# Attention through memory slots with a mixture of depths: factor stores on ScalarE in a new layout, row loads shared by SP and POOL, the mean added on VectorE

## The chip, the cores and the metric

The kernel runs on one core of a Trainium2 chip. A core has five engines that run their own instruction queues in order: TensorE (PE, with its weight loads PEld), VectorE (DVE), ScalarE (ACT), GpSimd (POOL) and SyncE (SP); transfers are done by 16 DMA engines, and each transfer is issued as an instruction in the queue of some engine. An order between engines exists only where one waits for a semaphore of another. The metric is the device time of one run in microseconds (us). The span, from the first to the last instruction of one profiled execution, is a little shorter than that execution's own device time.

## The reference

Sizes: B = 8 batches, H = 8 heads, S = 576 tokens, Dh = 64, M = 32 memory slots, D = 512, F = 1024, capacity 128; all float32.

```python
a    = softmax(phi, axis=2)                      # over the S tokens, for each of 32 slots
k_m  = einsum('bhsm,bhsd->bhmd', a, k)           # key means, 32 x 64 per head
v_m  = einsum('bhsm,bhsd->bhmd', a, v)           # value sums, 32 x 64 per head
x    = softmax(q @ k_m.T / 8, axis=-1) @ v_m     # then heads side by side: (B, S, 512)
scores  = x @ w_gate
top_idx = argpartition(-scores[b], 128)[:128]    # per batch
out     = x.copy()
out[b, top_idx] = x[top_idx] + sigmoid(scores[top_idx]) * (relu(x[top_idx] @ w1) @ w2)
```

The choice of the 128 tokens is made by comparing scores, so that x has to be computed more exactly than its own tolerance would ask; that is why the kernel splits its numbers into high and low parts.

## The kernel before

**Tiling and stages.** The 8 x 8 heads are 16 groups of 4 heads (batch b, half g). Four heads of 32 slots fill the 128 partitions, and S lies along the free dimension. A group passes these stages, each a Python generator whose `yield` ends a step:

- `softmax` (L187-282), the exponential worked out in many VectorE and ScalarE instructions on 128 x 576 tiles. L215, L245, L253, L262 and L278 are some of VectorE's; `dh` (L231), `vh` (L234), `y0` and `inv` are ScalarE's, all through the helper `act` (L181).
- `keys` (L306-337): TensorE transposes the factors a (L314), ScalarE copies them to SBUF (L316), VectorE splits them into `hi` (L320) and `lo` (L322). POOL then stores both to the DRAM buffer `aparts[4, B, 2, 2, S, M]` with eight DMAs (L325), one for each part and head, each of 576 contiguous pieces of 128 B. TensorE multiplies k with a in 24 matmuls (L331) for the key means, and ScalarE copies these to `kbd` (L336).
- `split_v` (L284-302) loads v of a group (`vb`, L291), splits it on VectorE (L294, L296), and stores the parts to the DRAM buffer `vparts` from POOL (L298). Its pool `vio` has two buffers for the first nine groups; later `vio2` has one and each group is done in two cuts.

**Value sums.** They are made for sets of SET = 2 batches (four groups), in pieces of T = 18 of the 576 rows: 32 pieces a set, 128 in all. `load_rows` (L341) reads a piece back from DRAM in five DMAs, all issued by SP: one of `v_rows` (L344, 64 partitions, 288 KB) and four of `a_rows` (L351, one per head, 36 KB each, 16 partitions). There are three buffers of each. `all_sums` (L355) loads up to three pieces ahead, and starts on a set when the youngest of its four groups was finished at least five turns ago (L367, `made + 5`). A piece is 72 small matmuls on TensorE (L382) that add into four accumulators; after a set ScalarE copies them to `v_m` (L393).

**Per batch.** When the sums of a batch are there, `attention` runs: `centre` (L405) subtracts means (L417 is one of its VectorE steps; POOL makes the casts `los`, L443 and L445), `scores` (L482) multiplies q with the key means and takes the exponential (`expm1`, L477 and L479), and `attend` (L527) multiplies by `v_m` (denominators L535, products L548), scales by the reciprocal on VectorE (L552), adds the mean's row (L555; on POOL while softmaxes are still running, which the variable `working` tells, and on VectorE after that), computes the gate's scores, and stores x to `out` (L560) and to the scratch buffer `xs` (L564) from POOL's queue. `rank` (L574, L601) finds each token's rank, `gather` (L611) fetches the 128 chosen rows by an indirect DMA of POOL (L630), and `ffn` (L636) does the two products (L654, L664) and scatters the result (L671). At the end a value is loaded that tells whether a general path, not taken here, must be run.

**What sets the order.** The program is scheduled by hand: each engine executes in the order in which the Python code emits. The main loop (L753-786) goes by turns. In a turn come: one step of a softmax or `keys`, where two chains of groups alternate (`order`, L112: groups 0, 2, 4, 6, 8, 9, ... 15 and groups 1, 3, 5, 7, so that from the eighth on a single chain runs); every fourth turn, or every second once attention has begun (`attend_all`), a step of `split_v` (L763); 12, 10 or 7 steps of the sums, two time steps of a piece each (`steps`, L730); a step of attention; and two of the feed-forward part. `load_phi` (L98), `load_k` (L102, called at L228 inside `softmax`) and `load_q` (L106, called at L683 between `scores` and `attend`) bring inputs in from SP's queue. At turn 40 the two weight matrices are loaded (L758, L759).

Of the kernel before, what the change touches and what calls it, by code (L numbers as in the profile page):

```python
# [39 lines left out]
def kernel(  # L40
# [26 lines left out]
    F = w1.shape[1]  # L67
    KD, KF = D // P, F // P
    SET = 2
    T = 18  # L70
    scale = 1.0 / Dh ** 0.5
    out_flat = out.rearrange("b s d -> (b s) d")

# [28 lines left out]
    def load_k(i, ch):  # L102
        ks[i] = exs[ch].tile([PT, NC, D // NG], F32, name="kb")
        nc.sync.dma_start(out=ks[i], in_=k[groups[i]])
# [82 lines left out]
    def softmax(i, ch):  # L187

        ex = exs[ch]

        def t(name, dtype=F32):

            return ex.tile([P, NC * P if name in WIDE else S], dtype, name=name)[:, :S]

        r = phis.pop(i)
        less_mx = ex.tile([P, 1], F32, name="mx")
        nc.vector.tensor_scalar(out=t("den"), in0=r, scalar1=-1.0, scalar2=None, op0=ALU.mult,
                                op1=ALU.min, accum_out=less_mx)
        nc.scalar.activation(r, r, AF.Identity, bias=less_mx)
        q = t("q", I16)  # L200
        act(q, r, LOG2E)
        yield
        for ln2 in (LN2_HI, LN2_LO):
            stt(out=r, in0=q, scalar=-ln2, in1=r, op0=ALU.mult, op1=ALU.add)

        rh, rl = t("rh", I16), t("rl")
        act(rh, r, 2.0 ** 11)
        num, den = t("num"), t("den")
        act(num, r, SQ[0], SQ[1], AF.Square)
        act(den, r, EXP_Q[2] * UP, EXP_Q[1] * UP)  # L210
        ends = t("lo"), t("big")
        act(ends[0], rh, -0.2734375 * UP * GRID, UP)
        act(ends[1], rh, UP * GRID / 4, EXP_P[1] * UP)
        yield
        stt(out=num, in0=num, scalar=SQ[2], in1=r, op0=ALU.add, op1=ALU.mult)  # L215
        act(num, num, 1.0, EXP_P[2] * UP)
        stt(out=rl, in0=rh, scalar=-GRID, in1=r, op0=ALU.mult, op1=ALU.add)

        def near(val, f, end):


            low = t("low")
            stt(out=low, in0=val, scalar=-f * UP, in1=r, op0=ALU.add, op1=ALU.mult)
            stt(out=low, in0=rl, scalar=f * UP, in1=low, op0=ALU.mult, op1=ALU.add)
            tt(out=val, in0=end, in1=low, op=ALU.add)

        yield
        load_k(i, ch)  # L228
        near(den, -0.2734375, ends[0])
        dh = t("dh", I16)  # L230
        act(dh, den, FINE)  # L231
        near(num, 0.25, ends[1])
        vh = t("vh", I16)
        act(vh, num, GRID)  # L234
        y0 = t("y0", I16)
        act(y0, r, 1.0, 14 * LN2, AF.Exp)
        inv = t("rl2")
        act(inv, r, INV[0], INV[1], AF.Exp)
        act(inv, inv, 1.0, INV[2] - 9 * LN2, AF.Exp)
        yield  # L240


        lo, big, low = t("lo"), t("big"), t("low")
        tt(out=low, in0=num, in1=rl, op=ALU.mult)
        stt(out=lo, in0=num, scalar=GRID, in1=vh, op0=ALU.mult, op1=ALU.subtract)  # L245
        tt(out=lo, in0=lo, in1=rh, op=ALU.mult)
        tt(out=big, in0=vh, in1=rh, op=ALU.mult)
        tt(out=low, in0=low, in1=lo, op=ALU.add)
        stt(out=num, in0=big, scalar=UP, in1=low, op0=ALU.add, op1=ALU.add)
        yield  # L250

        dl, p = t("lo"), t("big")
        stt(out=dl, in0=den, scalar=FINE, in1=dh, op0=ALU.mult, op1=ALU.subtract)  # L253
        tt(out=p, in0=y0, in1=dh, op=ALU.mult)
        tt(out=num, in0=num, in1=p, op=ALU.subtract)
        tt(out=dl, in0=y0, in1=dl, op=ALU.mult)
        tt(out=num, in0=num, in1=dl, op=ALU.subtract)
        two_q = t("den", I32)
        yield
        act(two_q, q, UP, 127 * UP, AF.Relu)  # L260
        tt(out=num, in0=num, in1=inv, op=ALU.mult)
        tt(out=num, in0=num, in1=y0, op=ALU.add)  # L262
        sm = ex.tile([P, 4], F32, name="sm")
        e = num
        stt(out=e, in0=num, scalar=FINE, in1=two_q.bitcast(F32),
            op0=ALU.mult, op1=ALU.mult, accum_out=sm[:, 0:1])

        nc.vector.tensor_scalar_add(sm[:, 0:1], sm[:, 0:1], 1e-9)
        nc.vector.reciprocal(sm[:, 1:2], sm[:, 0:1])
        nc.vector.tensor_single_scalar(sm[:, 2:3].bitcast(I32), sm[:, 0:1].bitcast(I32), -4096,  # L270
                                       op=ALU.bitwise_and)
        nc.vector.tensor_sub(sm[:, 3:4], sm[:, 2:3], sm[:, 0:1])
        nc.vector.tensor_scalar_mul(sm[:, 2:3], sm[:, 2:3], -1.0)
        a0 = t("vh", F16)
        nc.scalar.activation(a0, e, AF.Copy, scale=sm[:, 1:2])  # L275
        yield
        for part in (2, 3):
            stt(out=e, in0=a0, scalar=sm[:, part:part + 1], in1=e, op0=ALU.mult, op1=ALU.add)  # L278
        stt(out=e, in0=e, scalar=sm[:, 1:2], in1=a0, op0=ALU.mult, op1=ALU.add)  # L279
        soft[i] = e  # L280
        yield
        yield from keys(i, ch)

    def split_v(some, pool, cuts):  # L284

        n = 4 * S * Dh // P
        for b, g in some:
            for x0 in range(0, n, n // cuts):
                x = slice(x0, x0 + n // cuts)
                vb = pool.tile([P, n // cuts], F32, name="vb")  # L290
                nc.sync.dma_start(out=vb, in_=v[b, g, :, x])  # L291
                yield
                hi = pool.tile([P, n // cuts], F32, name="vhi")
                nc.vector.tensor_single_scalar(hi.bitcast(I32), vb.bitcast(I32), -4096,  # L294
                                               op=ALU.bitwise_and)
                nc.vector.tensor_sub(vb, vb, hi)  # L296
                for vp, src in enumerate((vb, hi)):
                    nc.gpsimd.dma_start(  # L298
                        out=vparts[b, g, :, vp].rearrange("w r s d -> w (r s d)")
                                               .rearrange("w (p x) -> p w x", p=P)[:, :, x],  # L300
                        in_=src.unsqueeze(1).to_broadcast([P, 2, n // cuts]))
                yield
# [3 lines left out]
    def keys(i, ch):  # L306
# [13 lines left out]
        nc.vector.tensor_single_scalar(hi.bitcast(I32), aS.bitcast(I32), -4096,  # L320
                                       op=ALU.bitwise_and)
        nc.vector.tensor_sub(lo, aS, hi)  # L322
        for part, src in enumerate((lo, hi)):
            for h in range(4):
                nc.gpsimd.dma_start(  # L325
                    out=aparts[h, b, g, part].rearrange("(c p) m -> p c m", p=PT),
                    in_=src[:, :, h * M:(h + 1) * M])
        km = bank([P, 2, 2 * M])
        for rr in range(2):
            for c in range(NC):  # L330
# [3 lines left out]
        for u in range(2):  # L334
            part = slice(u * Dh, (u + 1) * Dh)
            nc.scalar.activation(kbd[b][part, 2 * g:2 * g + 2, u * M:(u + 1) * M],  # L336
                                 km[part, :, u * M:(u + 1) * M], AF.Copy)

    accs = [accp.tile([P, 512], F32, name=f"acc{i}") for i in range(2 * SET)]

    def load_rows(k, st, ch):  # L341
# [4 lines left out]
            in_=vparts[some].rearrange("b g t w r s d -> (b g t w r) (s d)")  # L346
                [:, ch * T * Dh:(ch + 1) * T * Dh])
        for h in range(4):
            src = aparts[h, some].rearrange("b g t s m -> (b g t) (s m)")
            src = src[:, ch * T * M:(ch + 1) * T * M]  # L350
            nc.sync.dma_start(  # L351
                out=a_rows[k % 3][2 * h::8, h].rearrange("p s m -> p (s m)").bitcast(F32),
                in_=src.unsqueeze(1).to_broadcast([4 * SET, 2, T * M]))

    def all_sums():  # L355
# [7 lines left out]
        def load_some(end):  # L363
            while len(loaded) < min(end, len(pieces)):
                st, ch = pieces[len(loaded)]

                if not all(turn >= made.get(i, turn) + 5  # L367
                           for i in range(st * SET * NG, (st + 1) * SET * NG)):
                    break
                load_rows(len(loaded), st, ch)  # L370
# [156 lines left out]
    def attend(b, general):  # L527
        eT, tg = eTs[b % 2], tgs[b % 3]
        row, rest = mean[b]
        for c0 in range(0, NT, 2):  # L530
# [5 lines left out]
                                     rhs=heads_of, start=True, stop=True)  # L536
            if working:
                yield
            rd = step.tile([P, 2, H], F32, name="rd")[:, :cols]
            nc.vector.tensor_scalar(out=rd.rearrange("p c (g h) -> p c g h", g=2), in0=den,  # L540
                                    scalar1=float(M), scalar2=1e-9, op0=ALU.add, op1=ALU.add)
# [2 lines left out]
            for c in range(cols):  # L544
                o = bank([P, D])
                nc.tensor.matmul(out=o, lhsT=ones3, rhs=rest, start=True, stop=False)
                for g in range(2):
# [4 lines left out]
                nc.vector.tensor_mul(x[:, c].rearrange("p (h d) -> p h d", d=Dh),  # L552
                                     o.rearrange("p (h d) -> p h d", d=Dh),
                                     rd[:, c].unsqueeze(2).to_broadcast([P, H, Dh]))
            (nc.gpsimd if working else nc.vector).tensor_add(  # L555
                x, x, row.unsqueeze(1).to_broadcast([P, cols, D]))
            yield
            score(tg[:, c0:c0 + cols, 1], x, cols)
# [117 lines left out]
    def attention(b, general=False):  # L676
# [2 lines left out]
        yield from (scores_less_max if general else scores)(b)  # L679
        for j in range(2):  # L680
            yield
            if not general and b + 1 < B:
                load_q(b + 1, j)  # L683
        yield from attend(b, general)
        yield
        yield from rank(b)
# [66 lines left out]
    while True:  # L753
# [6 lines left out]
        if working and next(working[0], working) is working:  # L760
            finish(working[1])
            working.clear()
        if working and turn % (2 if attend_all else 4) == 1:  # L763
            next(working[1], None)
        for _ in range(steps()):
            next(sums, None)
        if attend_all is None and set(order[1]) <= set(made):
# [4 lines left out]
                ctx.enter_context(tc.tile_pool(name=name, bufs=2 - (name == "one"),  # L772
                                               reuse_waits="tile"))
                for name in ("step", "work", "one"))
            vio = ctx.enter_context(tc.tile_pool(name="vio2", bufs=1, reuse_waits="tile"))
            working[1] = split_v(groups[two + 1:], vio, 2)
            for j in range(2):
                load_q(0, j)
# [58 lines left out]
```

## Time and profile before

| | before |
|---|---|
| median of 3 runs (lowest to highest) | 908.98 us (899.76 to 917.44) |
| profiled execution: own time | 899.93 us |
| its span | 898.1 us |
| busy PE / PEld | 584.2 us (65%) / 427.7 us (48%) |
| busy DVE | 611.5 us (68%) |
| busy ACT / POOL | 295.3 us (33%) / 234.9 us (26%) |
| mean granted TensorE clock | 0.822 |
| moved by DMA | 166.10 MB, mean 185 GB/s |

The busy times are sums over the whole span, and the stages differ. The borders of the stages are events of the trace: the key means of groups 0 to 3 are ready at 49.4, 78.0, 106.5 and 135.0 us, the value sums of the four sets at 291, 431, 614 and 774 us, and the key means of the last group at 641 us. In a row of a group, "idle before" is the time for which the engine stood just ahead of these instructions, and the name after the arrow is what ended it. In a row of the timeline come the start, the duration, the engine and line, the operation with what it writes and reads, and in brackets the wait ahead of it and what ended that; a name ending in q (SPq) is a queue's issuing instruction.

### The profile page before, as it was taken

The numbers are of one execution on the slowest core, as the hardware profiler recorded it, in microseconds if no ns is written. First come the engines' busy times: TensorE is split into PE (matmuls) and PEld (weight loads), VectorE is DVE, ScalarE is ACT, GpSimd is POOL, SyncE is SP. The second block draws the span as 40 slices with busy tenths as digits, with TensorE's granted clock in tenths as the row PEclk, the third lists the DMA queues.
The fourth block names the chain that finished last, engine by engine and source line by source line (L and its number), as shares of the span: only waits on it lengthen the run. The fifth ranks groups of instructions, "written<-read, shape, count | busy, mean of one in ns | idle before, by whom it ended". The sixth has DMA issues, their size and how long they took to land. (4 is left out here: it accounts for less than half of the span.)

```text
span 898.1 us, 25253 instructions
## 1 busy us (share of the span) xinstructions
PE 584.2 (65%) x10738; PEld 427.7 (48%) x10738; DVE 611.5 (68%) x1117; ACT 295.3 (33%) x578; POOL 234.9 (26%) x349
## 2 busy tenths in 40 slices
PE   0122322556764646695847889867889989888794
PEld 0012222456653535574714557555556577544441
DVE  4899888857874765779789685979845333537820
ACT  3434434324441513332433624343331310332130
POOL 7033311330220432151423314232511010112200
PEclk9999999757585776886667979985899977989597
DMA  6367936876857786788554778664256566123300
GB/s 169 144 198 271 312 124 204 274 250 176 253 154 241 231 259 186 254 289 254 181 186 139 221 210 256 201 191 138 71 171 195 181 202 204 58 77 117 117 25 15
DMA packets 61944, 166.10 MB, mean 185 GB/s; under 512 B 11136, under 2 KB 21376, under 8 KB 61824
## 3 DMA queue, kind: packets, MB, share of 16 engines
q1 hardware_dynamic: 40096, 94.14, 34.8%
q0 software_dynamic: 21728, 70.27, 23.7%
q8 instruction: 87, 1.43, 0.7%
q14 instruction: 33, 0.27, 0.1%
HBM read 96.21 MB, written 68.16 MB: 183 GB/s over the span
## 5 line engine op out<-in xcount | busy, mean ns | idle before, releaser
L382 PE MATMUL acc<-a_rows,v_rows 32*64 32x128 f32 x9216 | 214.3, 253 | 127.8 <-DMA a_rows<-aparts 121.4
L382 PEld LDWEIGHTS acc<-a_rows,v_rows 32*64 32x64 f32 x9216 | 193.5, 162 | 170.4 <-issue 83.0
L314 PE MATMUL bank<-ident,num 128*96 128x128 f32 x96 | 21.3, 386 | 104.4 <-DVE num L279 99.4
L331 PE MATMUL bank<-lo,kb 96*128 96x64 f32 x384 | 64.5, 345 | 20.0 <-ACT lo L316 20.0
L331 PEld LDWEIGHTS bank<-lo,kb 96*128 96x128 f32 x384 | 62.7, 257 | 25.5 <-ACT lo L316 22.4
L325 POOL DMA_DIRECT2D aparts<-low x64 | 46.9, 740 | 104.8 <-DVE low L322 89.7
L298 POOL DMA_DIRECT2D vparts<-vb x23 | 16.9, 735 | 217.8 <-DVE vb L296 217.8
L654 PE MATMUL bank<-w_sb,xeT 128*128 128x512 f32 x128 | 69.8, 679 | 4.9 <-ACT xeT L645 3.2
L314 PEld LDWEIGHTS bank<-ident,num 128*96 128x96 f32 x96 | 15.4, 178 | 108.8 <-issue 88.4
L664 PE MATMUL bank<-w_sb,hT 128*128 128x512 f32 x128 | 60.8, 609 | 0.0
L548 PE MATMUL bank<-vbd,eT 128*128 128x256 f32 x160 | 58.3, 499 | 0.0
L552 DVE TENSOR_TENSOR xj<-bank,rd 128x512 f32<-128x512 f32 x40 | 27.5, 688 | 32.9 <-PE bank L548 32.4
L601 DVE SCALAR_TENSOR_TENSOR cmp<-row,tg,wide 128x576 bf16<-128x576 f32 x40 | 32.5, 814 | 24.0 <-ACT row L587 23.1
L325 POOL DMA_DIRECT2D aparts<-big x64 | 46.5, 734 | 3.8 <-DMA vparts<-vhi 3.7
L548 PEld LDWEIGHTS bank<-vbd,eT 128*128 128x128 f32 x160 | 34.1, 236 | 16.0 <-issue 12.1
L654 PEld LDWEIGHTS bank<-w_sb,xeT 128*128 128x128 f32 x128 | 25.3, 215 | 30.6 <-issue 22.1
L275 ACT ACTIVATE vh<-num,sm 128x576 f16<-128x576 f32 x16 | 12.4, 776 | 78.2 <-DVE sm L270 63.1
L555 POOL TENSOR_TENSOR xj<-xj,mean 128x1024 f32<-128x1024 f32 (+1 forms) x11 | 23.6, 2147 | 49.5 <-DVE xj L552 41.6
L479 DVE SCALAR_TENSOR_TENSOR eT<-es,th 128x288 f32<-128x288 f32 x32 | 14.4, 450 | 31.9 <-ACT th L477 31.9
L664 PEld LDWEIGHTS bank<-w_sb,hT 128*128 128x128 f32 x128 | 22.5, 189 | 25.9 <-issue 24.4
L336 ACT ACTIVATE kbd<-bank 64x64 f32<-64x64 f32 x32 | 7.0, 218 | 83.5 <-PE bank L331 83.3
L560 POOL DMA_DIRECT2D out<-xj x24 | 16.3, 678 | 66.8 <-DVE xj L555 63.8
(149 smaller groups left out, 1155.8 us busy)
## 6 DMA issues: line engine op xcount, KB each, us to landing
v_rows<-vparts SPq DMA_DIRECT2D x128, 288.0 KB
a_rows<-aparts SPq DMA_DIRECT2D x512, 36.0 KB
vparts<-vb POOLq DMA_DIRECT2D x9, 1152.0 KB, 5.5
vparts<-vhi POOLq DMA_DIRECT2D x9, 1152.0 KB, 8.7
kb<-in_k SPq DMA_DIRECT2D x16, 576.0 KB
qb<-in_qT SPq DMA_DIRECT2D x16, 576.0 KB
out<-xj POOLq DMA_DIRECT2D x16, 512.0 KB, 4.1
xs<-xj POOLq DMA_DIRECT2D x16, 512.0 KB, 4.3
```

The costliest lines, as they stand in the source:

```text
L298: nc.gpsimd.dma_start(out=vparts[b, g, :, vp].rearrange("w r s d -> w (r s d)") .rearrange("w (p x) -> p w x", p=P)[:, :, x], in_=src.unsq ...
L314: nc.tensor.transpose(out=tp[:, c], in_=a[:, (c0 + c) * PT:(c0 + c + 1) * PT], identity=ident)
L325: nc.gpsimd.dma_start(out=aparts[h, b, g, part].rearrange("(c p) m -> p c m", p=PT), in_=src[:, :, h * M:(h + 1) * M])
L331: nc.tensor.matmul(out=km[:, rr], lhsT=kb[:, c, rr * P:(rr + 1) * P], rhs=aS[:, c, rr * 2 * M:(rr + 1) * 2 * M], start=(c == 0), stop=(c = ...
L382: nc.tensor.matmul(out=accs[i][:Dh, :P].rearrange("p (h m) -> p h m", m=M), lhsT=vr[p, s], rhs=ar[p, :, s], start=(ch == 0 and s == 0), st ...
L548: nc.tensor.matmul(out=o[:, g * 4 * Dh:(g + 1) * 4 * Dh], lhsT=eT[:, g, (c0 + c) * P:(c0 + c + 1) * P], rhs=vbd[b % 3][:, g], start=False, ...
L552: nc.vector.tensor_mul(x[:, c].rearrange("p (h d) -> p h d", d=Dh), o.rearrange("p (h d) -> p h d", d=Dh), rd[:, c].unsqueeze(2).to_broadc ...
L555: (nc.gpsimd if working else nc.vector).tensor_add(x, x, row.unsqueeze(1).to_broadcast([P, cols, D]))
L560: nc.gpsimd.dma_start(out=out[b, c0 * P:c0 * P + (cols - 1) * P + n].rearrange("(c p) d -> p c d", p=n), in_=x[:n])
L601: nc.vector.scalar_tensor_tensor(out=cmp, in0=row, scalar=g, in1=wide[:, off:off + S], op0=ALU.is_equal, op1=ALU.mult, accum_out=equal[:, ...
L654: nc.tensor.matmul(out=ps[:n], lhsT=xeT[:, d, :n], rhs=w1_sb[:, d, f0:f0 + 512], start=(d == 0), stop=(d == KD - 1))
L664: nc.tensor.matmul(out=ps[:n], lhsT=hT[:, f, :n], rhs=w2_sb[:, f], start=(f == 0), stop=(f == KF - 1))
```

## The change

It has these parts.

- *Factors' layout and stores.* `aparts` becomes `(B, 2, 2, NC, 4, PT, M)`: batch, half, part, chunk of 96 rows, head, row, slot. The eight stores of a group become two, one per part, each from 96 partitions with 24 pieces of 128 B per partition. ScalarE issues them instead of POOL, and they stand after the copies to `kbd` instead of before the key matmuls.
- *Row loads.* T goes from 18 to 16, so that a piece lies within a chunk of 96 rows, and there are 36 pieces a set, 144 in all. Of the four `a_rows` loads of a piece, heads 0 and 1 stay on SP and heads 2 and 3 go to POOL; `v_rows` stays on SP. A set may start four turns after its last group, not five.
- *The split of v.* Its stores go from POOL to ScalarE, a turn's `yield` stands between the subtraction and the stores, `vio2` has two buffers, and once attention runs its steps come in two turns of three (before: one of two); ahead of that, one of three (before: one of four).
- *The mean.* L555 is a VectorE instruction throughout.
- *Input loads.* `load_k` is called one step later in `softmax`; `load_q` of the next batch is called inside `attend`, after its first denominators.

```diff
-    T = 18
+    T = 16
+    assert PT % T == 0
...
         yield
-        load_k(i, ch)
         near(den, -0.2734375, ends[0])
...
         stt(out=num, in0=big, scalar=UP, in1=low, op0=ALU.add, op1=ALU.add)
         yield
+        load_k(i, ch)
...
                 nc.vector.tensor_sub(vb, vb, hi)
+                yield
                 for vp, src in enumerate((vb, hi)):
-                    nc.gpsimd.dma_start(
+                    nc.scalar.dma_start(
...
         nc.vector.tensor_sub(lo, aS, hi)
-        for part, src in enumerate((lo, hi)):
-            for h in range(4):
-                nc.gpsimd.dma_start(
-                    out=aparts[h, b, g, part].rearrange("(c p) m -> p c m", p=PT),
-                    in_=src[:, :, h * M:(h + 1) * M])
         km = bank([P, 2, 2 * M])
...
                                  km[part, :, u * M:(u + 1) * M], AF.Copy)
+        for part, src in enumerate((lo, hi)):
+            nc.scalar.dma_start(
+                out=aparts[b, g, part].rearrange("c h p m -> p (c h) m"),
+                in_=src.rearrange("p c (h m) -> p (c h) m", m=M))
...
         for h in range(4):
-            src = aparts[h, some].rearrange("b g t s m -> (b g t) (s m)")
-            src = src[:, ch * T * M:(ch + 1) * T * M]
-            nc.sync.dma_start(
+            src = aparts[some, :, :, ch * T // PT, h].rearrange("b g t p m -> (b g t) (p m)")
+            src = src[:, ch * T % PT * M:(ch * T % PT + T) * M]
+            (nc.sync if h < 2 else nc.gpsimd).dma_start(
                 out=a_rows[k % 3][2 * h::8, h].rearrange("p s m -> p (s m)").bitcast(F32),
                 in_=src.unsqueeze(1).to_broadcast([4 * SET, 2, T * M]))
...
-                if not all(turn >= made.get(i, turn) + 5
+                if not all(turn >= made.get(i, turn) + 4
...
             if working:
                 yield
+            if c0 == 0 and not general and b + 1 < B:
+                for j in range(2):
+                    load_q(b + 1, j)
...
-            (nc.gpsimd if working else nc.vector).tensor_add(
+            nc.vector.tensor_add(
                 x, x, row.unsqueeze(1).to_broadcast([P, cols, D]))
...
         for j in range(2):
             yield
-            if not general and b + 1 < B:
-                load_q(b + 1, j)
...
-        if working and turn % (2 if attend_all else 4) == 1:
+        if working and (turn % 3 if attend_all else turn % 3 == 1):
             next(working[1], None)
...
-            vio = ctx.enter_context(tc.tile_pool(name="vio2", bufs=1, reuse_waits="tile"))
+            vio = ctx.enter_context(tc.tile_pool(name="vio2", bufs=2, reuse_waits="tile"))
...
-    aparts = nc.dram_tensor("aparts", (4, B, H // 4, 2, S, phi.shape[3]), F32, kind="Internal").ap()
+    aparts = nc.dram_tensor("aparts", (B, H // 4, 2, NC, 4, PT, phi.shape[3]), F32, kind="Internal").ap()
```

## The prediction, made before the changed kernel was run

> **What bounds the kernel now.** I read the busy time by stage first. The stage borders are events in the trace: key means of the first four groups ready (L336 at 135 us), set sums done (L393 at 291, 431, 614 and 774 us), last softmax done (641 us).
>
> ```profile
> core 0: us, PE busy (x) PEld busy (x) DVE busy (x) ACT busy (x) POOL busy (x), PEclk, DMA share, GB/s
> 0.00:137.00 137.00, 27.51 (x120) 24.98 (x120) 110.52 (x172) 55.51 (x89) 47.41 (x92) 1.00 0.62 201
> 137.00:291.00 154.00, 83.20 (x2432) 76.26 (x2433) 113.32 (x184) 51.66 (x83) 31.35 (x45) 0.70 0.73 224
> 291.00:431.00 140.00, 93.43 (x2499) 77.87 (x2498) 103.19 (x191) 46.25 (x92) 42.10 (x58) 0.73 0.77 241
> ...
> 460.00:614.00 154.00, 119.30 (x2613) 83.68 (x2611) 123.69 (x227) 61.58 (x121) 51.46 (x63) 0.86 0.68 207
> ...
> 650.00:776.00 126.00, 117.32 (x2566) 81.63 (x2565) 51.50 (x108) 25.93 (x67) 16.25 (x27) 0.89 0.60 181
> 776.00:898.00 122.00, 94.00 (x328) 50.20 (x326) 58.41 (x140) 32.61 (x77) 18.18 (x31) 0.84 0.20 65
> ```
>
> To 641 us the softmax chain on VectorE sets the pace (110 of 137 us, then 113 of 154); after that TensorE does (117 of 126). VectorE has slack between 137 and 614 us. Where it goes is seen by following its longest idle stretch back, from the stretches of the timeline on VectorE, ScalarE and TensorE:
>
> ```profile
> 197.44 0.48 PE L382 MATMUL acc<-a_rows,v_rows 32*64 32x128 f32 x8 [7.76 <-DMA a_rows<-aparts]
> 203.27 0.45 ACT L336 ACTIVATE kbd<-bank 64x64 f32<-64x64 f32 x2 [15.51 <-PE bank L331]
> 205.03 0.76 DVE L245 SCALAR_TENSOR_TENSOR lo<-num,vh 128x576 f32<-128x576 f32 x1 [10.87 <-ACT vh L181]
> ```
>
> A row load comes late, TensorE stands at the sums (L382), the key matmuls queued behind them are late, ScalarE stands at the copy L336, and VectorE at L245. And the rows are late because SP's queue does nothing but issue:
>
> ```profile
> 211.87 0.50 SPq L344 DMA_DIRECT2D v_rows<-vparts  x1
> 212.41 2.45 SPq L351 DMA_DIRECT2D a_rows<-aparts  x4
> 214.96 0.50 SPq L344 DMA_DIRECT2D v_rows<-vparts  x1
> 215.51 2.44 SPq L351 DMA_DIRECT2D a_rows<-aparts  x4
> ```
>
> A piece every 3.1 us, of which 2.95 is issue. Adding up VectorE's idle stretches over 1 us from 137 to 641 us by their releasers, about 56 us hang on rows in this way (10.9, 4.6, 7.8, 2.9, 2.1, 11.2, 2.6, 3.1, 6.4, 4.9 us), 9 us on vb from HBM (4.9, 1.6, 2.6), and 6.7 us on POOL's add (2.5, 4.2).
>
> **What the Trainium skill says.** Perfetto Trace Analysis, "DMA Instruction — HWDGE (DVE, Sync)": an SP or ACT queue is held until all descriptors of its DMA are generated, and the two share one generator. The trace before agrees so far as it goes: a load with 512 contiguous pieces (qb, 128 partitions x 4) holds SP for 0.6 us, one with 1024 (w2, L759) for 1.16:
>
> ```profile
> 82.83 1.16 SPq L759 DMA_DIRECT2D w_sb<-in_w  x1
> ...
> 364.40 0.61 SPq L108 DMA_DIRECT2D qb<-in_qT  x1
> ```
>
> Against it: w1 (L758), also 512 pieces but of 4 KB, held it for 1.19. SBUF — State Buffer, "Who interferes with whom": a VectorE instruction with two SBUF inputs contends with a GpSimd one that reads SBUF. The trace agrees: L215 takes 0.76 us by its median, and beside POOL's add
>
> ```profile
> 397.40 2.36 POOL L555 TENSOR_TENSOR xj<-xj,mean 128x1024 f32<-128x1024 f32 x1 [4.01 <-DVE xj L552]
> 397.92 2.46 DVE L215 SCALAR_TENSOR_TENSOR num<-num,ph 128x576 f32<-128x576 f32 x1 [0.61 <-ACT num L181]
> ```
>
> DMA: Bandwidth & Descriptors, "Issuing engines are not separate DMA queues": more issuers save issue time only. Here issue time is what is short, so the split can help.
>
> **The change, part by part.** Sums are against the profiled execution, 899.9 us (span 898.1 and 1.8 around it). The median of the runs, 909.0, is 1.01 times that.
>
> *Row loads and T = 16.* SP issues 128 x (0.50 + 4 x 0.61) = 376 us of row loads now and 144 x (0.50 + 2 x 0.61) = 248 us then; per piece 1.7 us where 3.1 were, while a piece is 2/18 smaller. POOL gets 288 issues. It shows none of this shape; its direct DMAs last 0.55 to 0.74 us (L560's smallest, L325), so 158 to 213 us, which takes the place of 93 (L325) + 34 (L298) + 24 (L555) = 151 us. Busy is not its limit; order is: a row load now stands in POOL's queue behind `out` stores that wait for VectorE, and the `los` casts (L443), stores and gathers stand behind row loads that wait for TensorE to free a buffer. Three buffers, some two turns of 4 to 5 us, cover a landing of about 4 us (last a_rows issue at 664.64, use at 668.69). From both sides: all 56 us back, or none. I take 70%, because the DMA engines, busy 0.73 to 0.77 of these stages, get denser when these get shorter: -16 us to 291 us (of 23) and -23 after (of 33). TensorE's last set of sums, 650 to 776 us, has 9 us of idle in all: -5.
>
> *Factor stores.* POOL loses 128 stores of 576 pieces of 128 B; ScalarE gets 32 of 2304 (96 partitions x 24). Nothing in the trace is issued by ScalarE. By 1.13 ns a piece (1.16 us over 1024) one holds it for 2.6 us; lower bound 0.6, what small SP loads take, if pieces don't count; upper 3.7, if 144 small writes for each DMA engine hold generation back. A saving on ScalarE is excluded, since it only gains work. I take 2.6. They stand after L336 and before `dh` and `vh`, and there is no slack there:
>
> ```profile
> 106.49 0.45 ACT L336 ACTIVATE kbd<-bank 64x64 f32<-64x64 f32 x2 [4.43 <-PE bank L331]
> ...
> 107.72 0.68 ACT L181 ACTIVATE vh<-num 128x576 int16<-128x576 f32 x1
> ...
> 108.43 0.76 DVE L245 SCALAR_TENSOR_TENSOR lo<-num,vh 128x576 f32<-128x576 f32 x1
> ```
>
> ScalarE would be free again at 106.94 + 5.3 = 112.2, `dh` and `vh` (1.27 us) end at 113.5, and L245 starts 5.1 us later, with VectorE idle. In the first stage three such cycles: +15. In the second, five, less 2.9 us of slack at 161 us: +23. Then seven with one chain, whose next user is `ph` of the next group; attention's work covers a quarter, so 3.8 each: +27. At the last group the stores end at 641.5 + 5.3 = 646.9 where POOL ended at 650.4, but set 3's sums stand behind feed-forward matmuls until 660.9: nothing.
>
> *v stores.* 46 DMAs of 256 pieces on ScalarE, 0.5 us each by SP's v_rows, 23 pairs. The added yield puts them after the subtraction, so ScalarE rarely waits for it; I take 0.4 us of each pair as exposed: +9 (+3 to 291 us, +6 after). Waiting behind them: the exponentials and copies that VectorE needs. Bounds 0 and +23.
>
> *The mean's add.* Eleven POOL adds go. Eight of them stretch a VectorE instruction by 1.3 to 2.2 us (L215 twice, L245, L253, L262, L278, L417 twice), 15.1 us together, and two more make VectorE wait 6.7. VectorE pays 8 x 1.23 + 3 x 0.69 = 11.9 (its own adds in L555). -9.9 us, and gone if the stretched instructions were waiting for something else anyway.
>
> *The small ones.* Two vb buffers end SP's waits for vparts stores (105 us in 6 waits) and VectorE's 9 us for vb: -5 to 291 us, -4 after. load_k and load_q move by a turn and issue the same 16 + 16 DMAs, 0.43 and 0.60 us on SP, which no longer is full: nothing; if SP stays full, 2 to 5 us. Rows one turn earlier after a set's last group: nothing, see the last group.
>
> Sum: +15; +23 - 16 - 5 + 3 = +5; +27 - 23 - 4 - 10 + 6 = -4; -5. Together **+11, 911 us** in the profiled execution, and times 1.01 **920 us** beside the median.
>
> **The rivals.** *(1) Cheap stores, faster.* If piece count doesn't matter, 0.6 us: ScalarE is back at 108.2, L245 slips 1.1 us. +3; +5.5 - 16 - 5 + 3; +6 - 23 - 4 - 10 + 6; -5, together about -39: 861, beside the median **870 us**. For it: w1 against w2, and 295 KB is a small transfer. Against: qb and w2.
>
> *(2) POOL in order, slower.* Place: 137 to 614 us. Row loads behind POOL's waits for VectorE arrive as late as SP's did, so TensorE's 105 us at a_rows between 137 and 431 us stay, and 16 + 23 + 5 = 44 us of gain go: 955, beside the median **965 us**. It decides from where less than a third of the row stalls go, and then the kernel is over 2% slower. For it: POOL already waits 63.8 us for L555 ahead of `out` and 53.5 ahead of `los`. Against: TensorE itself can't pass VectorE's position by much, since the transposes L314 wait for it.
>
> *(3) The split doesn't spread anything*, since transfers, not issue, limit: then pieces stay at 3.1 us with SP's queue idle between them. The time is near (2)'s.
>
> **How the numbers follow.** The main case 0.52, cheap stores 0.26, (2) with (3) 0.22. The main case runs from 895 to 948 (recovery of 50 to 100%, stores of 2.0 to 3.3 us); it is within 2% in most of its width. Range: from cheap stores with nearly all rows recovered, 866, to rival (2), 962. 2% is about what a measurement of this kernel can tell from no change (its three runs span 899.8 to 917.4). Faster by over 2% (below 891): the first rival and a little of the main case, 0.28. Slower (over 927): the second and a third of the main case, 0.40. Within: 0.32.
>
> **What would show it.** Right: ScalarE's queue with stores of about 2.6 us after L333 of the changed file, VectorE idle some 5 us before L245, groups 33 us apart in the first stage (28.5 now); SP's a_rows two by two with gaps; TensorE's wait for a_rows down from 121 us to some 40; no VectorE instruction of 2 us and more. Wrong: stores under 1.2 us, or TensorE's waits unchanged, or a wait for POOL on TensorE's `los` transposes.

## The result: slower by 4.4%

The changed kernel takes 942.46 us (median of four runs, 940.26 to 949.37) against 905.9 us before (four runs as well); the ratio is 1.044, with a 95% interval from 1.034 to 1.054. Medians here and below are of all runs of a kernel; the ratios leave out those that fell into a slower state of the chip. The profiled execution spans 938.5 us. The forecast was 920 us, within 2% of before; the time lies in its range (866 to 962), near the upper end of its main case (895 to 948). Of the three outcomes it held slower by over 2% the likeliest, at 0.40.

The profile after, busy time of each engine by stage, with the borders at the same events as before (key means of group 3, then the sums of the four sets):

```profile
core 0: us, PE busy (x) PEld busy (x) DVE busy (x) ACT busy (x) POOL busy (x), PEclk, DMA share, GB/s
0.00:139.00 139.00, 27.50 (x120) 24.96 (x120) 108.88 (x170) 53.78 (x86) 16.39 (x50) 1.00 0.57 176
139.00:304.00 165.00, 79.52 (x2424) 73.87 (x2424) 112.74 (x181) 52.29 (x85) 42.93 (x79) 0.69 0.71 214
304.00:455.00 151.00, 95.19 (x2507) 79.64 (x2508) 99.31 (x189) 45.96 (x90) 46.61 (x85) 0.71 0.72 219
455.00:653.00 198.00, 149.20 (x2701) 105.68 (x2700) 148.14 (x284) 76.17 (x154) 60.84 (x102) 0.78 0.68 206
653.00:809.00 156.00, 138.79 (x2662) 93.43 (x2662) 79.55 (x170) 34.21 (x89) 60.60 (x106) 0.88 0.51 157
```

VectorE's busy time is nearly what it was (607 us in all for 612); what the stages between 139 and 653 us gained in length is idle time. By events, with the best relative of the changed kernel beside it (stores on POOL, below):

| us | before | after | stores on POOL |
|---|---|---|---|
| key means of group 3 | 135.0 | 138.6 | 130.3 |
| sums of set 0 | 291.0 | 303.6 | 272.5 |
| sums of set 1 | 430.7 | 455.3 | 415.5 |
| sums of set 2 | 614.0 | 652.9 | 612.5 |
| key means of group 15 | 641.1 | 684.7 | 642.2 |
| sums of set 3 | 774.3 | 807.5 | 768.3 |
| span | 898.1 | 938.5 | 893.8 |

Of the 43.6 us at group 15, 3.5 were lost to 139 us; the rest came in the stages with row loads. (Against the relative with its stores on POOL, 8.3 us were lost by then.) TensorE's wait for rows grew instead of shrinking. The costliest waits of TensorE for rows, before and after, from the groups of the pages (the columns: busy time and mean, then the idle time ahead of the instructions and what ended most of it):

```profile
L382 PE MATMUL acc<-a_rows,v_rows 32*64 32x128 f32 x9216 | 214.3, 253 | 127.8 <-DMA a_rows<-aparts 121.4
```

```profile
L383 PE MATMUL acc<-a_rows,v_rows 32*64 32x128 f32 x9216 | 211.2, 253 | 171.5 <-DMA a_rows<-aparts 163.1
```

163 us where it was 121. The view of the line that issues these loads (L352) tells the two issuers apart; for SP's, and then for POOL's, it lists who waited how long, and how often:

```profile
L352 SPq DMA_DIRECT2D a_rows<-aparts x288: 574/590/2196, 144.9 to 801.4; - x144
...
  PE acc L383: 158.8, 50
```

```profile
L352 POOL DMA_DIRECT2D a_rows<-aparts x288: 540/556/857, 145.3 to 800.3; - x144
...
  PEld acc L383: 63.3, 21
  PE acc L383: 4.2, 3
```

So the loads that hold TensorE's matmuls up are mostly the two that stayed on SP, whose queue was relieved, and not those that went to POOL. What SP's queue waited for (total, times, longest):

```profile
SPq L345 <- PE acc L383: 134.5, 61, 17.4
SPq L352 <- DMA aparts<-big: 100.1, 8, 47.1
...
SPq L352 <- DMA vparts<-vb: 55.2, 7, 14.7
SPq L292 <- DMA vparts<-vb: 42.3, 4, 14.8
...
SPq L345 <- DMA vparts<-vhi: 22.7, 9, 7.6
```

The first line is a wait for a free buffer, and most of the second is the start of a set. But the third can't be a dependence on data: a load of `a_rows` reads `aparts` and writes a row buffer, and it waits here 55 us for stores of `vparts`. The longest of these waits, in the timelines of SP, ScalarE, TensorE and VectorE:

```profile
213.86 0.50 SPq L345 DMA_DIRECT2D v_rows<-vparts  x1
224.01 0.68 ACT L182 ACTIVATE rh<-ph 128x576 int16<-128x576 f32 x1 [2.41 <-DVE ph L205]
224.73 0.38 ACTq L300 DMA_DIRECT2D vparts<-vb  x1
229.11 1.72 SPq L352 DMA_DIRECT2D a_rows<-aparts  x2
232.54 1.76 PE L383 MATMUL acc<-a_rows,v_rows 32*64 32x128 f32 x56 [12.72 <-DMA a_rows<-aparts]
236.45 0.49 ACT L318 ACTIVATE lo<-bank 96x384 f32<-96x384 f32 x1 [9.09 <-PE bank L316]
237.61 0.56 DVE L322 TENSOR_SCALAR big<-lo 96x768 int32<-96x768 int32 x1 [10.79 <-ACT lo L318]
```

SP stands from 214.4 to 229.1 us. The store of `vb` waits in ScalarE's order until 224.7, behind `rh`, which waits for VectorE; it lands some 4 us later, and only then SP issues the row load. TensorE stands 12.7 us, and then the transposes behind it, ScalarE's copy and VectorE (10.8 us). The compiled program shows why. Each DMA of SP or ScalarE reports its completion on one of eight semaphores, which are handed out in turn, in the order of the program, to both engines together (all 632 such DMAs of the program, without exception). This is how the program was compiled. The trace agrees: its 584 executed DMAs of SP and ScalarE report on eight numbers, POOL's 352 on eight others. A DMA that takes a semaphore waits, where its engine can't know it already, for the one that had it before, eight DMAs earlier:

```
DMA  semaphore
103  6   ScalarE L300 vparts <- vb      (the store at 224.73)
104  7   SP      L352 a_rows
105  0   SP      L105 kb
106  1   ScalarE L300 vparts <- vhi
107  2   SP      L345 v_rows
108  3   SP      L352 a_rows
109  4   SP      L352 a_rows
110  5   SP      L345 v_rows            (issued at 213.86)
111  6   SP      L352 a_rows            (waits for 103; issued at 229.11)
```

In the program of before, ScalarE issues no DMA, and none of SP's waits for one of ScalarE's; in the changed program 60 do. In the trace, the store at 224.73 and the load at 229.11 carry one semaphore number, and SP's wait that ends at 229.06 is for that number. This was theory A when the experiments began: SP's queue is tied to ScalarE's place in the program, and thereby to VectorE's.

### The profile page after: what moved, and what is told of

Same layout as the page of the kernel before. It is cut to its first block, busy times and chain, and to the rows that moved or that the text cites. A ratio compares the mean times of both kernels' runs of the same rounds, so it can differ in the third digit from the quotient of the medians.

```text
span 938.5 us, 25316 instructions
## 1 busy us (share of the span) xinstructions
PE 586.8 (63%) x10738; PEld 428.7 (46%) x10738; DVE 607.4 (65%) x1128; ACT 295.2 (31%) x578; POOL 245.4 (26%) x452
## 4 chain that ended last, share of the span: by engine, by line
DVE 31%; PE 29%; DMA 18%; ACT 7%; issue 5%; ACTq 4%; SPq 2%; POOL 2%; DVEq 0%; POOLq 0%
PE acc L383 7%; DMA a_rows<-aparts 6%; PE bank L668 5%; DMA vparts<-vhi 5%; PE bank L328 4%; PE bank L658 4%; ACTq L336 3%; DMA aparts<-big 3%; PE bank L552 3%; DVE ph L205 1%; PE bank L491 1%; PE bank L536 1%; DVE low L224 1%; DVE low L225 1%; DVE vb L297 1%
## 5 line engine op out<-in xcount | busy, mean ns | idle before, releaser
L383 PE MATMUL acc<-a_rows,v_rows 32*64 32x128 f32 x9216 | 211.2, 253 | 171.5 <-DMA a_rows<-aparts 163.1
L352 POOL DMA_DIRECT2D a_rows<-aparts x288 | 161.0, 566 | 490.1 <-PE acc L383 336.0
L658 PE MATMUL bank<-w_sb,xeT 128*128 128x512 f32 x128 | 71.7, 695 | 4.8 <-ACT xeT L649 3.9
L552 PEld LDWEIGHTS bank<-vbd,eT 128*128 128x128 f32 x160 | 33.7, 234 | 16.5 <-issue 12.7
L322 DVE TENSOR_SCALAR big<-lo 96x768 int32<-96x768 int32 x16 | 8.8, 552 | 45.4 <-ACT lo L318 45.4
L205 DVE SCALAR_TENSOR_TENSOR ph<-q,ph 128x576 f32<-128x576 int16 x32 | 24.1, 752 | 17.8 <-ACT q L182 17.3
L318 ACT ACTIVATE lo<-bank 96x384 f32<-96x384 f32 x32 | 14.4, 483 | 58.2 <-PE bank L316 58.0
L603 ACT ACTIVATE sign<-row,tg 128x576 bf16<-128x576 f32 x40 | 30.9, 774 | 4.4 <-issue 2.5
```

The costliest lines, as they stand in the source:

```text
L352: (nc.sync if h < 2 else nc.gpsimd).dma_start(out=a_rows[k % 3][2 * h::8, h].rearrange("p s m -> p (s m)").bitcast(F32), in_=src.unsqueeze ...
L383: nc.tensor.matmul(out=accs[i][:Dh, :P].rearrange("p (h m) -> p h m", m=M), lhsT=vr[p, s], rhs=ar[p, :, s], start=(ch == 0 and s == 0), st ...
L552: nc.tensor.matmul(out=o[:, g * 4 * Dh:(g + 1) * 4 * Dh], lhsT=eT[:, g, (c0 + c) * P:(c0 + c + 1) * P], rhs=vbd[b % 3][:, g], start=False, ...
L603: nc.scalar.activation(sign, row, AF.Sign, bias=g, scale=-1.0, accum_out=less[:, c:c + 1])
L658: nc.tensor.matmul(out=ps[:n], lhsT=xeT[:, d, :n], rhs=w1_sb[:, d, f0:f0 + 512], start=(d == 0), stop=(d == KD - 1))
```

## The experiments

Ratios are against runs of the kernel before on the same chip, with 95% intervals. A hundredth is 9 us.

**Stores on POOL.** The same kernel with both kinds of stores issued by POOL, whose DMAs report on semaphores of their own.

```diff
-                    nc.scalar.dma_start(
+                    nc.gpsimd.dma_start(
                         out=vparts[b, g, :, vp]...
-            nc.scalar.dma_start(
+            nc.gpsimd.dma_start(
                 out=aparts[b, g, part]...
```

> The changed kernel with both kinds of stores (factors and v, new layout, new places) issued by POOL instead of ScalarE. Theory A (completion semaphores: a DMA of SP waits for the DMA issued eight before it in program order by SP or ScalarE, so SP's row loads stand behind ScalarE's stores, which stand behind VectorE): SP's waits for vparts at L345 and L352, 86 us in the changed kernel, go; TensorE's wait for SP's a_rows falls from 159 us to under 90; ScalarE no longer is held (L245's waits of 1.5 to 4.5 us are gone); time 890 to 915. Rival B (row loads in POOL's order are late): POOL has more to wait for, the loads it issues are later, TensorE's wait for POOL's a_rows rises from 67 us to over 120, time 940 or more.

897.72 us, ratio 0.984 (0.979 to 0.990): six hundredths below the changed kernel, and one and a half below the kernel before. SP's waits for `vparts` at L345 and L352 went from 86 us to 2.4, and TensorE's for SP's loads from 159 to 81; the view of L352 for SP:

```profile
L352 SPq DMA_DIRECT2D a_rows<-aparts x288: 574/590/2498, 136.0 to 761.7; - x144
...
  PE acc L383: 81.0, 33
```

The wait for POOL's loads rose as far as rival B has it, from 67 to 134 us (from 4.2 to 40.8 on the matmuls, 63.3 to 92.8 on the weight loads, which overlap with them), but the time fell, against rival B. What cost six hundredths is thus that ScalarE issues the stores, not the layout, their place or the split.

**The split, undone in the changed kernel.**

```diff
-            (nc.sync if h < 2 else nc.gpsimd).dma_start(
+            nc.sync.dma_start(
```

> The changed kernel with all four row loads of a piece on SP. Theory A: SP is as full as before the change and is still held by ScalarE's stores, so TensorE's wait for a_rows grows to 190 us or more and the time is 955 to 985. Rival B (POOL's order is the trouble): the time falls to 925 or less.

1017.22 us, 1.113 (1.109 to 1.118), worse than theory A expected; TensorE's wait for rows is 204 us. So POOL's order isn't what made the changed kernel slow; the split helps it by seven hundredths.

**Small DMAs beside the stores of before.** The kernel before with 78 more DMAs, once from ScalarE and once from POOL.

```diff
                         in_=src.unsqueeze(1).to_broadcast([P, 2, n // cuts]))
+                small(vb)       # nc.scalar (or nc.gpsimd).dma_start of src[:1, :16] to scratch
+                small(hi)
...
                                  km[part, :, u * M:(u + 1) * M], AF.Copy)
+        small(lo[:, 0])
+        small(hi[:, 0])
```

> The kernel before, unchanged in its own stores, with additional DMAs of 64 B from ScalarE to a scratch buffer, two after each group's kbd copies and two after each subtraction in split_v, reading the tiles that the changed kernel's stores read. Theory A: SP shows waits for these DMAs at L344, L351 of 40 us or more, TensorE's wait for a_rows grows from 121 to over 150 us, time 925 to 950 although they move 5 KB in all. Rival C (what costs is that ScalarE is held by large stores, or the transfers): 900 to 915, SP has no such wait.

> Control for the run with small DMAs on ScalarE: the same DMAs of 64 B issued by POOL, 78 of some 0.6 us. SP does not wait for them; Theory A: 900 to 918, TensorE's wait for a_rows 115 to 130 us. If it is as slow as the one on ScalarE, the wait for the tiles or the number of DMAs is what costs, not the engine that shares semaphores with SP.

924.83 us, 1.011 (1.007 to 1.015) from ScalarE, and 964.08 us, 1.057 (1.050 to 1.065) from POOL: the control was slower than the test, against theory A as it was put. The waits of SP tell why the pair decides nothing. These DMAs read `vb` and so keep its buffer, and SP's next load of `vb` waits for that, the row loads behind it. In the one from POOL:

```profile
SPq L297 <- DMA scrap<-vb: 129.1, 10, 34.0
```

From ScalarE this line has 50.6 us, and row loads waited 16 us for the small DMAs, where theory A asked for 40. The pair was made again without the buffer.

**Small DMAs that hold nothing.** The kernel with its stores on POOL, and at each of the 78 places of a store a DMA of 64 B from a constant tile, once from ScalarE, once from SP.

```diff
+    def small():
+        nc.scalar.dma_start(out=scrap[len(used):len(used) + 1], in_=ident[:1, :16])   # or nc.sync
+        used.append(1)
```

> The changed kernel with its stores on POOL (897.7 us in the first batch), and at each of the 78 places where the changed kernel had a store on ScalarE a DMA of 64 B from a constant tile to a scratch buffer, issued by ScalarE. It reads nothing that is waited for and holds no buffer. Theory A (SP's DMAs wait for ScalarE's DMA eight before, by a shared semaphore): SP shows waits for these at L345/L352 of 40 us or more, and the time goes most of the way back, 920 to 942. Theory D (the changed kernel lost its time because ScalarE was held by the large stores): 897 to 905, ScalarE's 78 issues cost 0.3 us each with slack beside them.

> Control: the same 78 DMAs of 64 B from the constant tile in the same places of the program, issued by SP. No DMA of SP then stands behind another engine's. Theory A: 895 to 907, no waits for the scratch buffer. If it is as slow as the one on ScalarE, the number of DMAs is what costs.

From ScalarE 921.05 us, 1.011 (1.003 to 1.019); from SP 900.23 us, 0.991 (0.988 to 0.995). The same number of DMAs in the same places, 5 KB in all, costs two hundredths when it is ScalarE that issues them. SP's waits for these DMAs in the first, at row loads and at `kb` (none is listed in the second):

```profile
SPq L360 <- DMA scrap<-ident: 34.2, 8, 11.7
...
SPq L111 <- DMA scrap<-ident: 4.0, 1, 4.0
```

With 1.7 us at L353 this makes 36 us at row loads, a little under the 40 that theory A asked for; the time is at the lower end of what it gave. In the compiled programs 61 DMAs of SP wait for one of ScalarE's in the first, none in the second. TensorE's wait for rows, from ScalarE and from SP:

```profile
L391 PE MATMUL acc<-a_rows,v_rows 32*64 32x128 f32 x9216 | 214.2, 256 | 158.6 <-DMA a_rows<-aparts 145.4
```

```profile
L391 PE MATMUL acc<-a_rows,v_rows 32*64 32x128 f32 x9216 | 218.8, 258 | 130.1 <-DMA a_rows<-aparts 119.6
```

That ScalarE itself is held by the 78 issues (0.26 us by the median) explains little of it: at the key means of group 3, before the first load of `a_rows` but after 17 of the small DMAs, the two kernels are 1.1 us apart (131.4 and 130.3 us), and at those of group 15 they are 19.5 us apart (666.2 and 646.7). That shared semaphores cost time is thereby shown; this is about two of the six hundredths. The true stores can cost more by it, since they wait for VectorE's subtraction and take 4 us to land.

**Which stores.** One kind at a time back to POOL.

> The changed kernel with only the v stores moved to POOL; the factor stores stay on ScalarE. Splits the 44 us between the two kinds. Theory A: the v stores are the later ones in ScalarE's order and SP waited 86 us for them against 7 us for the factor stores outside a set's start, so this takes back most: 900 to 918. Theory D: it takes back little, 925 to 940.

> The changed kernel with only the factor stores moved to POOL; the v stores stay on ScalarE. Theory A: 920 to 940, the waits of SP for vparts remain. Theory D (ScalarE held for 2.4 us by each pair of factor stores, VectorE late at L245): 900 to 915.

With the v stores on POOL 914.97 us, 1.010 (1.007 to 1.013); with the factor stores on POOL 932.68 us, 1.023 (1.011 to 1.034). Both lie where theory A has them: some three and a half hundredths hang on the v stores, two on the factor stores. Theory D has a share in it all the same, for the factor stores. Where the v stores stay on ScalarE, SP's waits for `vparts` at row loads stay (83 us). Where the factor stores stay, these are gone, but VectorE waits 37.1 us at L245 for `vh` (10.2 with all stores on POOL), since ScalarE is held by their issue. When the time is lost tells the two apart. In all these runs the first load of `a_rows` comes at 136 us or later, and the key means of group 3 are ready at:

| stores on ScalarE | none | v | both kinds | factors |
|---|---|---|---|---|
| key means of group 3, us | 130.3 | 130.3 | 138.6 | 147.1 |
| key means of group 15, us | 642.2 | 669.1 | 684.7 | 654.7 |

The v stores cost nothing as long as no rows are loaded, and 26.9 us by group 15: they cost by way of SP. The factor stores alone cost 16.8 us before any row load and less than that (12.5) at group 15: they cost by holding ScalarE. In the changed kernel this part is 8.3 us, and VectorE's waits at L245 in the first stage make 8.1 (there are none with all stores on POOL):

```profile
53.86 0.76 DVE L245 SCALAR_TENSOR_TENSOR lo<-num,vh 128x576 f32<-128x576 f32 x1 [1.51 <-ACT vh L182]
83.91 0.76 DVE L245 SCALAR_TENSOR_TENSOR lo<-num,vh 128x576 f32<-128x576 f32 x1 [3.00 <-ACT vh L182]
114.01 0.76 DVE L245 SCALAR_TENSOR_TENSOR lo<-num,vh 128x576 f32<-128x576 f32 x1 [3.56 <-ACT vh L182]
```

The two factor stores of a group in the changed kernel, duration as lowest, median, highest in ns:

```profile
L336 ACTq DMA_DIRECT2D aparts<-low x16: 311/328/340, 48.4 to 684.8; - x16
L336 ACTq DMA_DIRECT2D aparts<-big x16: 361/2066/3778, 48.7 to 685.1; - x16
```

and with the v stores on POOL:

```profile
L336 ACTq DMA_DIRECT2D aparts<-low x16: 311/311/362, 48.4 to 654.8; - x16
L336 ACTq DMA_DIRECT2D aparts<-big x16: 1952/2284/9161, 48.8 to 655.1; - x16
```

**The mean's add alone**, L555 on VectorE in the kernel before.

> The kernel before with the mean's add on VectorE throughout, nothing else. The prediction priced this at -9.9 us, and at nothing if the stretched instructions were waiting for something else anyway. Expected from its theory 896 to 904 us with the eight instructions of 2 us and more gone; from its rival (VectorE isn't the limit there) 904 to 912.

895.58 us, 0.983 (0.976 to 0.990). The longest L215 is 761 ns, where it was 2465. VectorE's busy time falls by 3.8 us (611.5 to 607.7) although it now makes all these additions, and its 6.7 us of waits for POOL's add are gone. TensorE's wait for rows falls too, from 121 to 98 us; why, this run doesn't tell. This part is a gain, and as large as that of the whole change with its stores on POOL.

**The split where nothing is shared.** Stores on POOL, all row loads on SP; and, the other way round, the kernel before with the mean's add on VectorE and the split, with T = 18, the old layout and the old stores.

> The changed kernel with its stores on POOL (897.7 us) and, in addition, all four row loads of a piece back on SP. This gives the worth of the split of the row loads where no semaphore is shared between engines. The prediction took SP's issue time for the limit and the split to be worth 44 us: 930 to 950. Rival E (transfers or buffers limit, the split is worth little): 895 to 910.

> The kernel before with the mean's add on VectorE and the a_rows of heads 2 and 3 issued by POOL; T stays 18, the factor stores stay in POOL with the old layout, v stores on POOL, one vio2 buffer. The split alone, on top of 895.6 us. If the split's gain stands by itself, as the prediction had it (some 40 us), 850 to 870; if POOL is then too full (128 factor stores of 0.74 us and 256 row loads of 0.56 us) or another wait is next, 885 to 905, which is also where the changed kernel with its stores on POOL is.

The first takes 952.06 us, 1.048 (1.040 to 1.055), 2 us above what the prediction's view gave: there the split is worth six hundredths. The second takes 908.69 us, 1.000 (0.996 to 1.005), above both of the ranges given: there the split costs nearly two. TensorE's waits in the second, for SP's row loads and for POOL's:

```profile
  PE acc L382: 30.6, 18
```

```profile
  PEld acc L382: 98.0, 25
  PE acc L382: 92.3, 16
```

Now POOL's loads are late, and what POOL stands at, besides buffers, is the v stores, queued in the turn in which VectorE makes their data:

```profile
POOL a_rows L351 <- PE acc L382: 198.0, 63, 10.8
POOL vparts L298 <- DVE vb L296: 120.5, 14, 17.5
```

In the changed kernel with its stores on POOL the same wait has 23.3 us; its v stores stand a turn after the subtraction. That the added `yield` makes this difference is argued, not shown: it wasn't tried alone, and the two kernels differ in T and layout as well. POOL's waits for VectorE's data at the factor stores are longer there, 92.4 us against 35.4.

**A candidate**, T = 12 and four row buffers, stores on POOL.

> A candidate: the changed kernel with its stores on POOL, pieces of T = 12 rows and four row buffers instead of three of 16 rows, in the same memory. If TensorE's 122 us at a_rows come from loads that start too late for want of a free buffer, 880 to 893; if from the number of DMAs and their issue, 900 to 915.

892.13 us, 0.984 (0.977 to 0.991), the lowest median of all, and not to be told from the stores on POOL with three buffers. TensorE's wait for rows is 110.5 us there, where it is 121.7 with three. T and the number of buffers changed together, so this run doesn't tell what limits the loads.

## Why the prediction was right or wrong

The sum gave +11 us on the profiled execution; the measured difference of the two is 40 us. It forecast a little slower, and it was slower, but the sum's terms went apart. That the time lies in the range is in part luck: a cost put at 65 us came out much smaller, a gain of 44 us did not come, and the mechanism that cost the most was in none of the cases.

*Row loads and T = 16: the step that failed.* It said that the split takes 44 us of stalls away, some 70% of them, and left the rest to denser transfers. TensorE's wait for rows rose to 163 us instead of falling to some 40. Issue time on SP was indeed short, and the split is worth what the step said where nothing else changes (six hundredths, 57 us). Three things stood against it. SP got another wait, for ScalarE's stores; the prediction looked at which queue each DMA moves to, and took it that a DMA waits only for data and buffers. Then, the comparison was with T = 18: with all loads on SP and no shared semaphores, the kernel with T = 16 is at 1.048, and the one of before with the mean's add moved is at 0.983. The two differ in more than T; but 16 more pieces at some 2.9 us of SP's issue come to 46 us, as an estimate, about what the split then pays back. That T is the cause wasn't tested. So even with its stores on POOL the changed kernel (0.984) gains nothing over the add alone (0.983), and TensorE's wait there, 121.7 us, is that of before, now with SP itself waiting 186 us for free buffers.

Third, POOL's order. With its stores on POOL the changed kernel is some 18.5 us ahead of the one before at the sums of set 0, earlier than any add of the mean, and only 1.5 us ahead at the sums of set 2. In the last stretch of these, 415 to 612 us, POOL's queue also has attention's work, and TensorE's matmuls wait 6.5 us for SP's loads but longer for POOL's:

```profile
L352 POOL DMA_DIRECT2D a_rows<-aparts x72: 537/569/807, 438.0 to 601.3; - x72
...
  PEld acc L383: 30.0, 10
  PE acc L383: 22.9, 6
```

In the kernel before, the matmuls waited 9.3 us for the `a_rows` loads of this stage (431 to 614 us) and the weight loads 7.4. That the split gains early and loses here fits rival 2; no run tried it alone.

*Factor stores: mechanism right, size off.* Priced at 2.6 us a store, 5.2 a pair, by pieces; they take 0.33 and 2.07 us. VectorE's wait at L245 is 24.9 us in all, where 13.7 were there before, and not 65 more. Groups in the first stage are 30.1 us apart, not 33 (28.5 before); the term for that stage, 15 us, measured 8.3 against the kernel with its stores on POOL. In all, moving these stores back to POOL saves two hundredths, 19 us.

The price by pieces, drawn from the two loads with 512 and 1024, doesn't hold: of two stores alike, with 2304 each, the first leaves in 0.33 us and the second takes 2.07.

*v stores: the wrong path.* +9 us, as ScalarE's own time at 0.5 us a store. The issue does take 0.38 and 0.48 us by the median of its two kinds; but putting them back on POOL saves 3.4 hundredths, 31 us: SP's waits for `vparts` at row loads end, and TensorE's wait for rows falls from 163 to 124 us.

*The mean's add.* -9.9 us; alone it measured -1.7 hundredths, 15 us (interval 9 to 22). VectorE's own saving in the profiles is 10.5 us (3.8 of busy time, 6.7 of waits). This agrees with the Trainium skill, SBUF — State Buffer, "Who interferes with whom", by which a VectorE instruction with two inputs in SBUF contends with a GpSimd one that reads SBUF: without POOL's adds L215 never exceeds 0.76 us.

*The small ones.* SP's wait at the loads of `vb` fell from 105 to 45 us and didn't end (30 us with the stores on POOL). VectorE's own waits for `vb`, 10 us in all before, were to go and rose to 17.

*The rivals.* Cheap stores came half true, and the gain that was to follow did not. POOL's order (rival 2), at 965 us, was no nearer in time than the main case, and wrong in place: the matmuls waited 4 us for POOL's loads and 159 for SP's. In the kernel of before with the split, though, it is just what happens. Rival 3, that transfers and not issue limit, doesn't fit the runs with the stores on POOL: the same transfers take 0.984 with the split and 1.048 without it.

Of the 42.5 us by which the changed kernel is behind the one with its stores on POOL at group 15, 8.3 are thus ScalarE held by the factor stores in the first stage, and 26.9 are what the v stores cost alone. Some 7 us are left, as an estimate that takes the parts to add up; which of the two ways they were lost stays open.

## What to carry to other kernels

When a DMA moves to another engine's queue, look for what the two queues share, the completion semaphores too: a queue that ran ahead then waits for the engine that runs behind, and nothing in the data says so. In a profile it shows as a load that waits for the store of a tensor that it doesn't touch. And measure the parts alone: here one line was worth as much as all the rest at its best.

## What was not expected of the hardware

A store of 96 x 24 pieces of 128 B holds ScalarE's queue for 0.31 to 0.36 us when it comes first, and the next one like it for 0.36 to 9.2 us; the two longest, 9.2 and 6.6 us in the run with the v stores on POOL, began 1 and 4 us after POOL had issued v stores of 1152 KB each. From POOL each of them takes 1.2 us (1187 to 1399 ns), the same for both, where four with 576 pieces took 0.73 each. So the number of pieces alone doesn't tell what such a DMA costs its queue here. That the second waits for room behind the first, or behind POOL's stores, is argued, not shown.
